# Decode attention over a long cache: P*V with V as the stationary operand, and more rows of one V chunk kept on chip

## The chip, the cores and the metric

The kernel runs on one core of a Trainium2 chip. The metric is the time of one execution in microseconds of device time; the median of three runs is used.

## The reference

Two attention blocks and two small mixer-and-MLP blocks alternate over the same x, eight batch rows of one token each. Both attention blocks read the same K and V cache, so the cache is needed twice:

```python
def _A_setup():
    B, Sq, D = 8, 1, 448
    Hq, Hkv, Sk, Dh = 16, 8, 4096, 256
...
def _A_ref(x, k_cache, v_cache, wq, wo):
    q = (lambda x, *d: x.transpose(*d))((x @ wq).reshape(B, Sq, Hq, Dh), 0, 2, 1, 3)
    k = jnp.repeat(k_cache, rep, axis=1)
    v = jnp.repeat(v_cache, rep, axis=1)
    scores = jnp.einsum("bhqd,bhkd->bhqk", q, k) * (Dh ** -0.5)
    p = _softmax(scores, axis=-1)
    o = jnp.einsum("bhqk,bhkd->bhqd", p, v)
    return (lambda x, *d: x.transpose(*d))(o, 0, 2, 1, 3).reshape(B, Sq, Hq * Dh) @ wo
...
x = x + _A_ref(_layernorm(x, axis=-1), A_k_cache, A_v_cache, A_wq, A_wo)
x = x + _B_ref(_layernorm(x, axis=-1), B_w1, B_w2, B_w3, B_w4)
x = x + _A_ref(_layernorm(x, axis=-1), A_k_cache, A_v_cache, A_wq, A_wo)
x = x + _B_ref(_layernorm(x, axis=-1), B_w1, B_w2, B_w3, B_w4)
```

The data are bf16. With S = 1 the mixer of `_B_ref` has shifts that push every row out, so only its norms, `w3`, the gelu and `w4` are computed.

## The kernel before

One batch row has 8 KV heads, each with 4096 keys of 256 values. Two KV heads form a pair `gp` (four pairs), and the K or V of a pair is cut into four chunks `c` of 1 MB: 128 partitions with 16 rows `y` of 256 bf16 values each. Every chunk lives in one of 15 places of SBUF (`places`, `slots`).

The first attention block is pass 0 (`ps == 0`), the second pass 1. A batch row's pass 1 follows soon after its pass 0, and part of the cache stays on chip between the two. Eleven chunks keep their places (`kept`: all K chunks of pairs 3 and 2, and V chunks 1 to 3 of pair 3). One more V chunk (`inner`) is put into four PSUM banks by DVE transposes (`away`, L748) and brought back for pass 1 (`back`, L755). Of one more V chunk (`part`, the first of pair 3) four of the 16 rows go into a fifth bank, `store[4]` (L960, back at L978); its load of pass 1 brings the other 12 rows, 768 KB.

`tasks` is the order of (pass, row, pair) written out by hand, and `items` cuts it into chunks: K chunks of a task alternate with the V chunks of the task before it. The main loop runs over `items`. For each item:

- A K chunk is transposed in place by DVE in three instructions (`transpose_k`, L713). Then PE makes the scores (`scores`, L728) with q as stationary operand and K moving; where two K chunks lie side by side one matmul takes both. ACT makes the exponentials and their sums (`exps`, L737), and PE and ACT turn the p of a whole task around (`transpose_p`, L764 and L771) into `ptw`.
- A V chunk goes through `pv` (L783): 16 matmuls, one for each row y, with 8 columns of `ptw` (two of them p, six zeros around) as stationary operand and the 256 values of V moving. Four rows y run at different 32-partition quadrants, and everything accumulates in one half of the PSUM bank `o` (`o_banks`), which has to be cleared before.
- Two pairs make a half. `half` (L445) sums and inverts the softmax denominators (`z_cols`, L414), copies the half bank out by ACT (L457), clears it by a DVE memset (L458), and folds the four quadrants, turns the result round and scales it in one step of four fp32 matmuls with `R` (L463). A DVE cast (L467) ends it.
- `pv_cols` (L797) is the form used for the last row's pass 1 of pairs 0 and 1: V as stationary operand, 128 columns at stride 2 for each of two column sets j, and two columns of p moving.

When an item is done its place is free (unless it is kept), and `emit_loads` issues as many of the coming loads as places allow, in the order of `items`, all on SP's queue (L700 for one chunk, L675 for two K chunks side by side). Each load waits on that queue until the last readers of its place have finished.

Everything else, output projection (L358), norms, MLP (L376), the next q (L309), is written as generators. `step` advances them between items at a pace given by the number of steps that they are said to have (`add_gen`, for instance 38 for `chain`) and by the item at which they have to be done.

Of the kernel before, what the change touches and what calls it, by code (L numbers as in the profile page):

```python
# [17 lines left out]
def kernel(  # L18
# [47 lines left out]
    part = (GP - 1, 1, 0)  # L66
    Q4 = 4 * Dh

# [23 lines left out]

    usel = consts.tile([128, 4], FP32, name="usel")
    for u in range(2):
# [6 lines left out]

    fold = consts.tile([128, 8], FP32, name="fold")
    nc.vector.tensor_reduce(
        fold[:],
        ident.rearrange("p (q n) -> p n q", q=4)[:, 0:8],
        mybir.AxisListType.X,
        ALU.add,
    )

    ptz = consts.tile([128, 520], BF16, name="ptw")  # L110
    nc.vector.memset(ptz[:], 0.0)
    ptw = ptz[:, 0:512].rearrange("p (a n w) -> p a n w", a=4, w=8)

    misc = psum.tile([128, 512], FP32, name="misc")
    ot_bank = misc[:, 256:320]
    sc = psum.tile([128, 512], FP32, name="sc")
    o_both = psum.tile([128, 512], FP32, name="o")
    o_banks = [o_both[:, 0:Dh], o_both[:, Dh : 2 * Dh]]
    store = [psum.tile([128, 512], FP32, name=f"store{n}") for n in range(5)]
    nc.vector.memset(sc[:], 0.0)  # L120
    nc.tensor.matmul(o_both[:], ptz[:, 0:128], ptz[:, 0:512], start=True, stop=True)

# [10 lines left out]

    wv = consts.tile([128, 4], FP32, name="wv")
    nc.vector.memset(wv[:, 0:3], 1.0 / D)
    nc.vector.memset(wv[0:64, 3:4], 0.0)
    nc.vector.memset(wv[64:128, 3:4], 1.0 / D)
    one = consts.tile([128, 1], FP32, name="one")
    nc.vector.memset(one[:], 1.0)
    ones = one[:].to_broadcast([128, 128])  # L140
    HTw = consts.tile([128, HC, Bn], BF16, name="HTw")
    nc.vector.memset(HTw[:], 0.0)
    low = consts.tile([128, 2, 4], FP32, name="low")
    for k, v in enumerate((1.0, (1 + EPS) ** -0.5)):
        nc.vector.memset(low[:, k], v)
        nc.vector.memset(low[0:64, k, 3:4], 0.0)
    eps2 = consts.tile([128, 2], FP32, name="eps2")
    nc.vector.memset(eps2[:, 0:1], EPS)
    nc.vector.memset(eps2[:, 1:2], EPS * EPS / (1 + EPS))
    nhalf = consts.tile([128, 1], FP32, name="nhalf")  # L150
    nc.vector.memset(nhalf[:], -0.5)
    xb = {}
    for nb in (1, Bn):
        xb[nb] = consts.tile([128, 5, nb], BF16, name=f"xb{nb}")
        nc.vector.memset(xb[nb][:, 3:5, :], 0.0)
# [47 lines left out]
    def norm(x, nb, twice):  # L203
# [15 lines left out]
        xx = room("xx", (2, 4), 0)  # L219
        nc.vector.tensor_mul(xx[:, 0], x, wv[:].unsqueeze(2).to_broadcast([128, 4, nb]))  # L220
        nc.vector.tensor_mul(xx[:, 1], xx[:, 0], x)
# [24 lines left out]
        def power(k0, k1):  # L246
            nc.gpsimd.tensor_tensor(  # L247
                rs[:, k0:k1].rearrange("p n b -> p (n b)"),
                ve[:, k0:k1].rearrange("p n b -> p (n b)"),
                nhalf[:].to_broadcast([128, (k1 - k0) * nb]),  # L250
                ALU.pow,
            )

        if twice and nb == 1:
            nc.vector.scalar_tensor_tensor(
                ve[:, :, 0], var.to_broadcast([128, 2]), 0.0, eps2[:], ALU.max, ALU.add
            )
            power(0, 2)
        else:
            if twice:  # L260
                nc.vector.tensor_scalar(
                    ve[:, 1], var, 0.0, EPS * EPS / (1 + EPS), ALU.max, ALU.add
                )
                power(1, 2)
            nc.vector.tensor_scalar(ve[:, 0], var, 0.0, EPS, ALU.max, ALU.add)
            power(0, 1)
# [147 lines left out]
    def z_cols(zall, gps):  # L414

        np_ = len(gps)
        zm = chn.tile([128, 4, np_], FP32, tag=f"zm{np_}")
        zs_t = chn.tile([128, 2], FP32, tag="zs")
        zs = zs_t[:, 0:np_]
        nc.vector.tensor_add(  # L420
            zs, zall[:, 0, gps[0] : gps[-1] + 1], zall[:, 1, gps[0] : gps[-1] + 1]
        )
        nc.vector.tensor_tensor(  # L423
            zm[:],
            zs.unsqueeze(1).to_broadcast([128, 4, np_]),
            usel[:].unsqueeze(2).to_broadcast([128, 4, np_]),
            ALU.mult,
        )
        yield
        z_ps = misc[:, 480 : 480 + 4 * np_].rearrange("p (n g) -> p n g", n=4)  # L430
        nc.tensor.matmul(z_ps, ones, zm[:], start=True, stop=True)  # L431
        yield
        rz = chn.tile([128, 4, np_], FP32, tag=f"rz{np_}")
        nc.vector.reciprocal(rz[:], z_ps)
        return rz

    def scale_o(o_ps, rz, gp, u, OT):

        h0 = 4 * gp + 2 * u
        for j in range(2):  # L440
            nc.vector.tensor_mul(
                OT[:, j, h0 : h0 + 2], o_ps[:, j, h0 : h0 + 2], rz[:, 2 * u : 2 * u + 2, 0]
            )

    def half(o_ps, zall, g8, OT):  # L445


        rz = yield from z_cols(zall, range(2 * g8, 2 * g8 + 2))

        R = chn.tile([128, 8], FP32, tag="R")  # L450
        nc.vector.tensor_mul(
            R[:].rearrange("p (g n) -> p g n", n=4),
            rz[:].rearrange("p n g -> p g n"),
            fold[:].rearrange("p (g n) -> p g n", n=4),
        )
        o_sb = chn.tile([128, Dh], FP32, tag="o_sb")
        nc.scalar.copy(o_sb[:], o_ps)  # L457
        nc.vector.memset(o_ps, 0.0)  # L458
        in_use[:] = [t for t in in_use if t is not o_ps]
        yield  # L460
        ot_ps = ot_bank[:, 32 * g8 : 32 * g8 + 16].rearrange("p (j h) -> p j h", j=2)
        for j in range(2):
            nc.tensor.matmul(  # L463
                ot_ps[:, j], o_sb[:].rearrange("p (i j) -> p j i", j=2)[:, j], R[:], start=True, stop=True
            )
        yield
        nc.vector.tensor_copy(OT[:, :, 8 * g8 : 8 * g8 + 8], ot_ps)  # L467
        yield

    in_use = []  # L470

# [188 lines left out]
    def emit_loads(most=None):  # L660
        n = 0
        while loads and places and n != most:
# [35 lines left out]
            if loads:  # L698
                z0 = Q4 if tasks[t][0] == 1 and halfway(it) else 0
                nc.sync.dma_start(dst[:, z0:], src[:, z0:])  # L700
# [51 lines left out]
    def back(slot):  # L752

        for n in range(4):
            nc.vector.transpose(  # L755
                slot[:].bitcast(U32)[:, 512 * n : 512 * n + 512], store[n][:].bitcast(U32)
            )

    def transpose_p(p_sb):

        pt_ps = misc[:, 0:128].rearrange("p (t k r) -> p t k r", t=4, k=4)
        cols = identb[:].rearrange("p (k r) -> p k r", k=4)[:, :, 0:8]
        for t in range(4):
# [7 lines left out]
        nc.scalar.copy(  # L771
            ptw[:, :, :, 6:8],
            pt_ps.rearrange("p t k (a h) -> p a (t k) h", a=4),
        )

    def pv(o_ps, v, a, gp):


        g = 2 * gp + a // 2
        for y in range(16):  # L780
            q = y % 4
            at = 128 * a + 8 * (4 * q + y // 4) + 6 - 2 * (g % 4)
            nc.tensor.matmul(  # L783
                o_ps[32 * q : 32 * q + 8, :],
                ptz[:, at : at + 8],
                v[:, y * Dh : (y + 1) * Dh],
                start=False,
                stop=(y >= 12),
                skip_group_check=True,
            )  # L790

    def pv_cols(o_ps, v, a, gp):

        g = 2 * gp + a // 2
        for y in range(16):
            for j in range(2):
                nc.tensor.matmul(  # L797
                    o_ps[:, j, 2 * g : 2 * g + 2],
                    v[:, y * Dh + j : (y + 1) * Dh : 2],
                    ptw[:, a, 4 * (y % 4) + y // 4, 6:8],  # L800
                    start=(a % 2 == 0 and y == 0 and j == 0),
# [57 lines left out]
    for idx, it in enumerate(items):  # L859
# [65 lines left out]
        else:  # L925
# [23 lines left out]
            else:  # L949
                g8 = gp // 2  # L950
                if ("o", g8) not in st:
                    while len(in_use) == 2:
                        step(10 * len(items))
                    st["o", g8] = next(t for t in o_banks if all(t is not u for u in in_use))
                    in_use.append(st["o", g8])
                pv(st["o", g8], slot, c, gp)
                if ps == 0 and inside(it):
                    away(slot)
                if ps == 0 and halfway(it):
                    nc.vector.transpose(store[4][:].bitcast(U32), slot[:, 0:Q4].bitcast(U32))  # L960
            if c == 3:
                done = pairs_done[ps, b] = pairs_done.get((ps, b), 0) + 1
                if done == 2 and ps == 0:
                    add_gen("chain", b, first_half(b, st), idx + 1, idx + (16 if b == 0 else 21), 10)
                elif done == 2:
                    add_gen("chain" if final else "last", b, first_last(b, st), idx + 1, idx + 13, 9)
                elif done == 4 and ps == 0:
                    add_gen("chain", b, chain(b, st), idx + 1, first_of[(1, b), 0] - 1, 38)
                elif done == 4 and not final:
                    add_gen("last", b, last(b, st), idx + 1, idx + (7 if b == Bn - 2 else 13), 6)  # L970
        if not (ps == 0 and stays(it)):
# [5 lines left out]
        if tasks[soon[0]][0] == 1 and halfway(soon):  # L977
            nc.vector.transpose(  # L978
                slots[where[soon]][:, 0:Q4].bitcast(U32), store[4][:].bitcast(U32)
            )  # L980
        emit_loads()
# [67 lines left out]
```

## Time and profile before

| What | Value |
|---|---|
| Time, median of 3 runs | 1098.04 us (1095.36 to 1102.22) |
| Span of the profiled execution | 1093.6 us |
| Its own time | not given by the page; the span is 4.4 us under the median |
| PE busy | 674.9 us (62%), 15063 matmuls and 15063 weight loads |
| DVE busy | 599.1 us (55%) |
| ACT busy | 125.9 us (12%) |
| Data moved | 446.80 MB, mean 409 GB/s |
| Mean granted TensorE clock | 0.593 |

Busy time is time in which at least one instruction of the engine runs, so matmuls that overlap are counted once. PE's matmuls and weight loads are separate rows (PE, PEld). A group of instructions is one line of the kernel, one operation and one shape; behind the bar stand its busy time, the mean duration of one in ns, and the idle time of the engine before it with what ended that. The 40 slices are 27.3 us each, and the digits tenths of busy time. "issue" is time in which an engine waited for nothing that the profile shows.

### The profile page before, as it was taken

How to read it: one execution, taken by the hardware profiler on the slowest of the kernel's cores; microseconds unless marked ns; L12 is line 12 of the kernel's file. 1: busy time of each engine (PE TensorE's matmuls, PEld its weight loads, DVE VectorE, ACT ScalarE, POOL GpSimd, SP SyncE). 2: the span in 40 equal slices, each digit the busy share in tenths (PEclk: the TensorE clock that was granted, in tenths of full speed). 3: DMA queues.
4: the chain of work that ended last, by engine and by line, in shares of the span. 5: the costliest groups of instructions: out<-in, count | busy, mean ns of one | idle time of the engine just before them, and what ended most of it. 6: DMA issues, size and time to landing. Idle time of an engine off the chain costs nothing. (4 is left out here: it accounts for less than half of the span.)

```text
span 1093.6 us, 32866 instructions
## 1 busy us (share of the span) xinstructions
PE 674.9 (62%) x15063; PEld 451.8 (41%) x15063; DVE 599.1 (55%) x1215; ACT 125.9 (12%) x362; POOL 16.3 (1%) x27
## 2 busy tenths in 40 slices
PE   3234568456864677446774467834776477767775
PEld 2123345334642355324552245522454244545554
DVE  4256564656366555555465564665637553585462
ACT  0001101110110111101021001201111101111110
POOL 0000000000000000000000000000000000000000
PEclk9986556655575556555566555665556555665565
DMA  9999999999999999999999999999999999999994
GB/s 356 394 427 419 416 403 420 420 416 407 418 423 419 406 417 422 423 419 402 419 422 423 420 401 418 423 421 417 411 416 421 420 398 419 421 411 409 421 417 188
DMA packets 62010, 446.80 MB, mean 409 GB/s; under 512 B 6568, under 2 KB 10544, under 8 KB 12336
## 3 DMA queue, kind: packets, MB, share of 16 engines
q1 hardware_dynamic: 61680, 444.32, 98.6%
q8 instruction: 118, 1.93, 0.7%
q10 hardware_dynamic: 192, 0.38, 0.2%
q14 instruction: 20, 0.16, 0.0%
HBM read 444.67 MB, written 0.01 MB: 407 GB/s over the span
## 5 line engine op out<-in xcount | busy, mean ns | idle before, releaser
L713 DVE STREAM_TRANSPOSE places<-places 128x512 uint32<-128x512 uint32 (+1 forms) x576 | 462.0, 858 | 263.1 <-DMA places<-in_A_k_cache_dram 262.7
L728 PE MATMUL sc<-places,qbd 128*8 128x128 bf16 (+1 forms) x6720 | 281.9, 309 | 217.8 <-DVE places L713 179.7
L783 PE MATMUL o<-places,ptw 128*8 128x256 bf16 x3968 | 241.9, 387 | 144.6 <-DMA places<-in_A_v_cache_dram 122.1
L728 PEld LDWEIGHTS <-qbd 128*8 128x8 bf16 x6720 | 161.2, 101 | 312.8 <-issue 136.8
L783 PEld LDWEIGHTS <-ptw 128*8 128x8 bf16 x3968 | 114.1, 109 | 192.2 <-issue 151.0
L737 ACT ACTIVATE p_n<-sc 128x256 bf16<-128x256 f32 x128 | 95.6, 747 | 763.1 <-PE sc L728 763.1
L309 PEld LDWEIGHTS <-wq_sb 128*128 128x128 bf16 x1152 | 36.0, 104 | 28.3 <-issue 18.4
L358 PEld LDWEIGHTS <-wo_sb 128*128 128x128 bf16 x1280 | 38.4, 102 | 19.8 <-issue 19.8
L332 DVE CAST qbd<-misc 32x64 bf16<-32x64 f32 x64 | 13.8, 216 | 55.6 <-PE misc L328 55.0
L309 PE MATMUL misc<-xb,wq_sb 128*128 128x1 bf16 x1024 | 34.5, 166 | 6.2 <-ACT ptw L771 3.2
L358 PE MATMUL misc<-OT,wo_sb 128*128 128x1 bf16 x1024 | 34.5, 165 | 1.2 <-issue 1.2
L737 ACT ACTIVATION_READ_ACCUMULATOR p_n<-sc 128x1 f32 x128 | 33.9, 265 | 0.0
L771 ACT CAST ptw<-misc 128x128 bf16<-128x128 f32 x64 | 17.4, 273 | 139.1 <-PE misc L764 79.1
L463 PEld LDWEIGHTS misc<-R,o_sb 128*128 128x128 f32 x124 | 26.1, 292 | 9.4 <-issue 8.6
L247 POOL TENSOR_TENSOR t<-t,nhalf 128x2 f32<-128x2 f32 (+2 forms) x20 | 14.0, 703 | 1064.9 <-DVE t L268 1064.9
L463 PE MATMUL misc<-R,o_sb 128*128 128x8 f32 x124 | 28.8, 342 | 0.1
L431 PE MATMUL misc<-zm,one 128*128 128x8 f32 (+1 forms) x66 | 18.5, 354 | 15.0 <-DVE zm L423 14.2
L755 DVE STREAM_TRANSPOSE places<-store 128x512 uint32<-128x512 uint32 x32 | 20.1, 684 | 10.7 <-PE sc L728 10.6
L431 PEld LDWEIGHTS misc<-zm,one 128*128 128x128 f32 x66 | 16.0, 300 | 21.5 <-issue 15.8
L376 PEld LDWEIGHTS <-w_sb 128*128 128x128 bf16 x560 | 17.2, 105 | 9.4 <-issue 9.2
L376 PE MATMUL misc<-xb,w_sb 128*128 128x1 bf16 (+1 forms) x560 | 18.5, 166 | 3.6 <-DVE xb L286 2.2
L748 DVE STREAM_TRANSPOSE store<-places 128x512 uint32<-128x512 uint32 x32 | 19.9, 690 | 0.9 <-DMA places<-in_A_v_cache_dram 0.8
(103 smaller groups left out, 241.9 us busy)
## 6 DMA issues: line engine op xcount, KB each, us to landing
places<-in_A_v_cache_dram SPq DMA_DIRECT2D x215, 1024.0 KB, 9.5
places<-in_A_k_cache_dram SPq DMA_DIRECT2D x146, 1024.0 KB, 9.9
places<-in_A_k_cache_dram SPq DMA_DIRECT2D x23, 2048.0 KB, 18.7
places<-in_A_v_cache_dram SPq DMA_DIRECT2D x8, 768.0 KB, 7.2
wo_sb<-in_A_wo_dram SPq DMA_DIRECT2D x1, 3584.0 KB, 27.5
wq_sb<-in_A_wq_dram SPq DMA_DIRECT2D x3, 1024.0 KB, 8.0
w_sb<-in_B_w_dram SPq DMA_DIRECT2D x1, 1568.0 KB
w_sb<-in_B_w_dram SPq DMA_DIRECT2D x3, 448.0 KB, 26.2
```

Source lines behind the costliest of these rows:

```text
L309: nc.tensor.matmul(q_ps[:, j * Hq + h, :], w, xbs(nb)[:, xi, :], start=(fc == 0), stop=(fc == 3),)
L358: nc.tensor.matmul(y_ps[:, fc, :], w[:, i, at : at + 128], rhs(i), start=start, stop=stop, skip_group_check=open is not None,)
L376: nc.tensor.matmul(h_ps[:, c * nb : c * nb + nb], w, xbs(nb)[:, xi, :], start=(fc == 0), stop=(fc == 3),)
L431: nc.tensor.matmul(z_ps, ones, zm[:], start=True, stop=True)
L463: nc.tensor.matmul(ot_ps[:, j], o_sb[:].rearrange("p (i j) -> p j i", j=2)[:, j], R[:], start=True, stop=True)
L713: nc.vector.transpose(w, w)
L728: nc.tensor.matmul(sc[32 * k : 32 * k + 8, 128 * x : 128 * (x + nx)], qbd[:, ep, gp].rearrange("p a h -> p (a h)"), v, start=(n == 0), sto ...
L737: nc.scalar.activation(p_sb[:, :, :, 2 * u : 2 * u + 2].rearrange("p t i x -> p x t i"), sc[:, 256 * u : 256 * u + 256].rearrange("p (x t ...
L748: nc.vector.transpose(store[n][:].bitcast(U32), slot[:].bitcast(U32)[:, 512 * n : 512 * n + 512])
L755: nc.vector.transpose(slot[:].bitcast(U32)[:, 512 * n : 512 * n + 512], store[n][:].bitcast(U32))
L771: nc.scalar.copy(ptw[:, :, :, 6:8], pt_ps.rearrange("p t k (a h) -> p a (t k) h", a=4),)
L783: nc.tensor.matmul(o_ps[32 * q : 32 * q + 8, :], ptz[:, at : at + 8], v[:, y * Dh : (y + 1) * Dh], start=False, stop=(y >= 12), skip_group ...
```

## The change

`pv` takes the form of `pv_cols`: for each of two column sets j and 16 rows y, 128 values of V at stride 2 are the stationary operand and the two columns of p move. That is 32 matmuls and 32 weight loads a chunk instead of 16 and 16, and the result lies as columns (head dimension on partitions), with start and stop of an accumulation for each chunk. A chunk of a pair has 4 output columns (two j, two heads), and the partial results of a half need 32 columns of the `o` bank instead of 256. So no clearing is needed, and `half` adds the two parts of each head (a DVE copy and an add) and multiplies by the inverse denominators; the ACT copy, the memset, `R` and the four fp32 matmuls are gone. Only one half at a time may be at work (`halves`).

The room that this leaves holds more of the `part` chunk: four rows in `store[4]` as before, three rows in the rest of the `o` bank, and four rows in a new SBUF tile `vx`, filled by an ACT copy and read by PV directly. `vx` finds its room because `ptw` shrinks to 128 columns and several small constants share one tile, `small`. The load of pass 1 brings five rows, 320 KB. The number of steps that the generators are said to have falls by two each.

```diff
-    Q4 = 4 * Dh
+    YS, YO, YX = 4, 3, 4
+    Y1 = YS + YO
+    YL = Y1 + YX
...
-    ptz = consts.tile([128, 520], BF16, name="ptw")
-    nc.vector.memset(ptz[:], 0.0)
-    ptw = ptz[:, 0:512].rearrange("p (a n w) -> p a n w", a=4, w=8)
+    ptw_t = consts.tile([128, 128], BF16, name="ptw")
+    ptw = ptw_t[:].rearrange("p (a n h) -> p a n h", a=4, h=2)
+    vx = consts.tile([128, YX * Dh], BF16, name="vx")
...
-    o_banks = [o_both[:, 0:Dh], o_both[:, Dh : 2 * Dh]]
+    o_sets = [o_both[:, 32 * k : 32 * k + 32] for k in range(2)]
+    o_rows = o_both[:, 512 - YO * 128 : 512]
...
-    def half(o_ps, zall, g8, OT):
+    def half(o_set, zall, g8, OT):
+        while halves:
+            yield
+        halves.append(g8)
         rz = yield from z_cols(zall, range(2 * g8, 2 * g8 + 2))
-        R = chn.tile([128, 8], FP32, tag="R")
-        nc.vector.tensor_mul(
-            R[:].rearrange("p (g n) -> p g n", n=4),
-            rz[:].rearrange("p n g -> p g n"),
-            fold[:].rearrange("p (g n) -> p g n", n=4),
+        parts = o_set.rearrange("p (j n a h) -> p a j n h", j=2, a=2, h=2)
+        o_t = chn.tile([128, 2, 8], FP32, tag="o_t")
+        o_v = o_t[:].rearrange("p j (n h) -> p j n h", h=2)
+        nc.vector.tensor_copy(o_v, parts[:, 0])
+        nc.vector.tensor_tensor(o_v, parts[:, 1], o_v, ALU.add)
+        in_use[:] = [t for t in in_use if t is not o_set]
+        nc.vector.tensor_tensor(
+            OT[:, :, 8 * g8 : 8 * g8 + 8],
+            o_t[:],
+            rz.rearrange("p g n -> p (g n)").unsqueeze(1).to_broadcast([128, 2, 8]),
+            ALU.mult,
         )
-        o_sb = chn.tile([128, Dh], FP32, tag="o_sb")
-        nc.scalar.copy(o_sb[:], o_ps)
-        nc.vector.memset(o_ps, 0.0)
-        in_use[:] = [t for t in in_use if t is not o_ps]
-        yield
-        ot_ps = ot_bank[:, 32 * g8 : 32 * g8 + 16].rearrange("p (j h) -> p j h", j=2)
-        for j in range(2):
-            nc.tensor.matmul(
-                ot_ps[:, j], o_sb[:].rearrange("p (i j) -> p j i", j=2)[:, j], R[:], start=True, stop=True
-            )
-        yield
-        nc.vector.tensor_copy(OT[:, :, 8 * g8 : 8 * g8 + 8], ot_ps)
+        halves.clear()
         yield
...
-                z0 = Q4 if tasks[t][0] == 1 and halfway(it) else 0
+                z0 = YL * Dh if tasks[t][0] == 1 and halfway(it) else 0
...
+    row_stores = [(0, YS, store[4][:]), (YS, Y1, o_rows)]
+    def rows_away(slot):
+        for y0, y1, t in row_stores:
+            nc.vector.transpose(t.bitcast(U32), slot[:, y0 * Dh : y1 * Dh].bitcast(U32))
+        nc.scalar.copy(vx[:], slot[:, Y1 * Dh : YL * Dh])
+    def rows_back(slot):
+        for y0, y1, t in row_stores:
+            nc.vector.transpose(slot[:, y0 * Dh : y1 * Dh].bitcast(U32), t.bitcast(U32))
...
-    def pv(o_ps, v, a, gp):
-        g = 2 * gp + a // 2
-        for y in range(16):
-            q = y % 4
-            at = 128 * a + 8 * (4 * q + y // 4) + 6 - 2 * (g % 4)
-            nc.tensor.matmul(
-                o_ps[32 * q : 32 * q + 8, :],
-                ptz[:, at : at + 8],
-                v[:, y * Dh : (y + 1) * Dh],
-                start=False,
-                stop=(y >= 12),
-                skip_group_check=True,
-            )
+    def pv(o_set, v, a, gp, kept_rows=None):
+        o_ps = o_set.rearrange("p (j g a h) -> p j g a h", j=2, g=2, a=4)
+        for j in range(2):
+            for y in range(16):
+                src, at = v, y
+                if kept_rows is not None and Y1 <= y < YL:
+                    src, at = kept_rows, y - Y1
+                nc.tensor.matmul(
+                    o_ps[:, j, gp % 2, a, :],
+                    src[:, at * Dh + j : (at + 1) * Dh : 2],
+                    ptw[:, a, 4 * (y % 4) + y // 4, :],
+                    start=(y == 0),
+                    stop=(y == 15),
+                )
...
                 if ps == 0 and halfway(it):
-                    nc.vector.transpose(store[4][:].bitcast(U32), slot[:, 0:Q4].bitcast(U32))
+                    rows_away(slot)
...
-                    add_gen("chain", b, chain(b, st), idx + 1, first_of[(1, b), 0] - 1, 38)
+                    add_gen("chain", b, chain(b, st), idx + 1, first_of[(1, b), 0] - 1, 36)
...
         if tasks[soon[0]][0] == 1 and halfway(soon):
-            nc.vector.transpose(
-                slots[where[soon]][:, 0:Q4].bitcast(U32), store[4][:].bitcast(U32)
-            )
+            rows_back(slots[where[soon]])
```

## The prediction, made before the changed kernel was run

> **What bounds the kernel now.** I read the busy shares and the DMA rows of the page first, then the windows by stage, then the chain that ended last, then the groups by shape. The DMA rows decide most of it.
>
> ```profile
> span 1093.6 us, 32866 instructions
> DMA  9999999999999999999999999999999999999994
> GB/s 356 394 427 419 416 403 420 420 416 407 418 423 419 406 417 422 423 419 402 419 422 423 420 401 418 423 421 417 411 416 421 420 398 419 421 411 409 421 417 188
> q1 hardware_dynamic: 61680, 444.32, 98.6%
> q8 instruction: 118, 1.93, 0.7%
> ```
>
> The DMA engines are busy in every slice but the last, at about 420 GB/s with a dip near 400 once in every 130 us or so, that is once a batch row. So the time is bytes over rate, and what the dips lose. Where the dips come from is seen when a batch row is cut in two, a stretch in which pass 2 and the kept chunks leave few free places, and one in which places are plentiful:
>
> ```profile
> 500.00:564.00 64.00, 50.06 (x1103) 33.63 (x1104) 34.65 (x83) 8.38 (x25) 1.26 (x2) 0.55 1.01 412
> 632.00:692.00 60.00, 45.95 (x938) 30.66 (x934) 30.47 (x76) 7.09 (x22) 1.25 (x2) 0.50 1.00 410
> 692.00:760.00 68.00, 35.17 (x758) 22.00 (x750) 40.45 (x62) 8.04 (x23) 0.00 (x0) 0.63 1.01 422
> ```
>
> The columns are PE, weight loads, DVE, ACT, POOL with their counts, then clock, DMA share, GB/s. In 632 to 692 a load lands 7.6 us (median) after its issue, in 692 to 760 21.5 us after: in the first there are some 1.5 MB on the way, in the second up to 9. Issued bytes less landed bytes, in 4 us slices of the trace, say what this costs: above 2 MB on the way the rate is 420 to 421 GB/s, at 1.4 to 1.6 MB 412, at 1.0 to 1.2 MB 397. The scarce slices add up to 476 us of the span. There the time hangs on how soon PE gives a place back.
>
> PE has a limit that is no busy share. In the chain of waits, at the densest place:
>
> ```profile
> 933.53 1.22 issue
> 934.76 0.48 PE misc L358 x13
> 935.24 0.13 PE misc L764 x4
> 935.39 0.28 ACT ptw L771
> 935.71 0.94 PE misc L358 x32
> 936.65 0.95 PE o L783 x16
> 937.61 1.77 PE misc L358 x63
> 939.38 1.59 issue
> 940.97 0.62 PE misc L358 x17
> ```
>
> Between the two "issue" gaps lie 13+4+32+16+63 = 128 matmuls with a weight load each: 256 instructions. PE's 15063 matmuls and 15063 weight loads at 64 bytes are 1.93 MB, which is the q8 row, and 1.93 MB in 118 packets is 16 KB, or 256 instructions, a packet. So these gaps are PE waiting for its next page of code. The page starts are 6.2 us apart here (934.76, 940.97), and of the 117 intervals between q8 packets 38 are under 6.6 us, in spite of a median of 8.2. I read a ceiling of 256 instructions in 6.2 us, 41 a us, while data transfers run.
>
> **The change, part by part.** *Fewer bytes.* Eight loads (768 KB, pass 2) become 320 KB: seven rows of 64 KB less, 3.67 MB in all. A packet of 6144 bytes takes 238 ns in the records; one of 2560 lies between 1792 bytes (80 ns) and 3584 bytes (146 ns), about 107 ns. 1024 packets x 131 ns / 16 engines = -8.4 us, if the engines stay fed.
>
> *PV on PE itself.* The shapes are in the trace already, since the last row of pass 2 does it at L797:
>
> ```profile
> L783 PE MATMUL o<-places,ptw 128*8 128x256 bf16 x3968 | 241.9, 387 | 144.6 <-DMA places<-in_A_v_cache_dram 122.1 <-issue 10.8 <-DVE o L458 9.3
> L463 PE MATMUL misc<-R,o_sb 128*128 128x8 f32 x124 | 28.8, 342 | 0.1
> L458 DVE MEMSET o<- 128x256 f32 x31 | 8.4, 272 | 12.3 <-ACT o_sb L457 11.1
> L797 PE MATMUL store<-ptw,places 128*128 128x2 bf16 x256 | 8.2, 166 | 2.3 <-DMA places<-in_A_v_cache_dram 2.3
> L797 PEld LDWEIGHTS <-places 128*128 128x128 bf16 x256 | 7.9, 106 | 3.1 <-DMA places<-in_A_v_cache_dram 2.7 <-issue 0.4
> ```
>
> Old: 241.9 / 248 chunks = 0.98 us. New: 8.2 / 256 = 32 ns a pair, 32 pairs, 1.03 us. That is a draw, +13 us of PE busy time in all, off the path. The Trainium skill (TensorE: Matmul & The Clock Gate, section LDWEIGHTS) speaks against this part: a weight load takes its columns over 1.2 ns, 107 ns for 128 against 7 ns for 8, which makes an estimate of 3.4 us a chunk. The L797 row has 31 ns of busy time for each such load, so the row is taken.
>
> *Instructions.* A chunk goes from 32 to 64 of them: 248 x 32 = 7936 more, less 31 x 8 for L463, so 7688 or 30 pages. As traffic a q8 packet lasts 1.06 us on one engine: 30 x 1.06 / 16 = +2.0 us (by bytes alone 1.2). As a ceiling it weighs more. 500 to 564 holds 2207 instructions, 272 of them PV matmuls: with 544 more and 24 less it needs 2727 / 256 x 6.2 = 66.0 us of its 64. 632 to 692: 1872 + 476 - 24 = 2324, 56.3 us of 60, where it was 45.3.
>
> What that costs no row shows. From below: nothing, where PE has waited for loads anyway (122.1 us before L783, 179.7 us at L728 for DVE). From above: in the scarce 476 us lie 3326 PV instructions, and as many new ones at 24.2 ns each are 80 us. To choose, I took the trace's PE start times, counted PV twice, and let a page arrive no sooner than 6.2 us after the page before it was begun: in the scarce slices PE is late by 0.56 us more than before in the mean, with peaks near 2 us. At 421 GB/s that is 0.24 MB less on the way, 1.2 instead of 1.45 MB, and by the rates above about 9 GB/s or 2.2% less over 476 us: +10 us. Just after the scarce stretch PE runs through kept chunks at full pace and the lateness grows to 5 to 9 us, where the loads on the way cover 2.5 to 4; pushing each issue back by it ends the loads about 5 us later, most of that in the last two batch rows: +4 us (0 to 9).
>
> The Trainium skill (Runtime: NRT & Kernel Launch, section Instruction fetch mechanics) also has blocks of 16 KiB fetched while the current one runs, but calls the cost of crossing mostly hidden; by that these two terms are nothing. The chain above, with 1.2 and 1.6 us of gap, says otherwise for dense stretches.
>
> *The end of a half.* The ACT copy (L457, 0.39 us), the memset and the four fp32 matmuls of L463 (28.8 / 31 = 0.93 us of PE) go; two short DVE operations on 16 columns and one product take the place of memset, R and cast. The DVE is 55% busy and gains nothing that counts. PE gets 0.93 us back, three times in a scarce stretch. None of it would be 0, all of it 8 x 3 x 0.93 = -22 us; by the same exchange rate as above, and because each lasts only a few us, -2 us.
>
> *Rows kept.* Eight times DVE moves 384 columns more out and in (0.72 us x 384/512 = 0.54 us each), and ACT copies 1024 columns: no row like it, between the 0.38 us of L457's 256 and four times that, 1.5 us. The move into the o bank also waits for PE, and the K transposes queue behind it. The place comes back later by 0 to 1.5 us, 0 to 12 us in all. SP waited for the old move only twice, 0.8 us, so +1 us.
>
> Sum: -8.4 + 2.0 + 10 + 4 - 2 + 1 = +6.6 us. The page gives the profiled execution's span alone, 1093.6 us; the median of the runs, 1098.0, is 4.4 above it, and I let that stay. 1098.0 + 6.6 = 1104.6, say 1105 us: hardly slower, within 1%. One per cent, 11 us, is about what a measurement of this kernel can tell from no change.
>
> **The rivals.** *Code pages stay hidden.* PE's slack in the scarce stretch, 14.7 us of 60, was larger than the 10.9 us added, and the fetch may start earlier when PE waits. Then -8.4 + 2.0 - 2 = -8.4 us: 1090 us. Against it: PE bunches its work, 195 instructions in 636 to 640, and waits between. A gain over 1% needs the dips to go too: 476 us at 411 instead of 421 GB/s hold 11 us, which would give 1079 at best.
>
> *PE's code becomes the bound of the scarce stretch.* This is the slower side. Each place hangs on PE's queue, and PE in turn on loads and DVE. If PE keeps up only 90% of 41 a us because of these waits, 632 to 692 needs 56.3 / 0.9 = 62.6 us and 500 to 564 needs 73.3, together 11.9 us more for two batch rows, or 45 for the seven and a half that are alike; with -8.4 + 2.0 that is 1136 us. At 95% only the second is longer, by 5.5 us, 21 in all, and 1112 us. It decides from about 93%, where the scarce stretch is longer than its transfers. Against it: places are given back at one a 1.6 us even at the ceiling, and a transfer takes 2.5.
>
> *The saved rows save nothing*, since the 320 KB load lies in the scarce stretch, where the engines already run dry. Then the -8.4 falls away: 1113 us. Loads of 8192 bytes in those slices still keep the engines at 1.00 to 1.02, so I give it little.
>
> **How the numbers follow.** Forecast, 1096 to 1109: 0.42. Pages hidden, 1081 to 1095: 0.27, a third of it below 1087. PE's code the bound, 1110 to 1140: 0.27. Rows that save nothing: 0.04. So faster by over 1%: 0.09; within 1%: 0.42 + 0.18 = 0.60, less 0.06 for the edge of the forecast towards 1110, 0.54; slower: 0.27 + 0.04 + 0.06 = 0.37. The range leaves a tenth at each end: 1087 to 1126.
>
> **What would show it.** Right: q8 near 148 packets and 2.4 MB, the DMA's total near 443.6 MB, PV rows at about 32 ns a pair; "issue" gaps before PV weight loads, ending 256 instructions apart and 6.2 us apart, over whole scarce stretches; the rate there at 400 to 405 GB/s and still 421 where places are plentiful. Wrong: scarce stretches at 412 or more with q8 packets 7 us apart (the first rival), or packets 6.2 us apart without a break and the rate below 390 (the second).

## The result, and the profile after

The changed kernel takes 1118.05 us (median of 4 runs, 1114.2 to 1120.4), the kernel before 1099.01 us (4 runs): a ratio of 1.0168, 95% interval 1.0142 to 1.0195. It is 19 us slower; 1105 were forecast. Its profiled execution is the run of 1114.2 us, with a span of 1112.3.

The page of the changed kernel, its span, rates and DMA queues:

```profile
span 1112.3 us, 40541 instructions
GB/s 359 396 426 419 401 409 385 420 408 392 395 425 420 397 417 402 424 417 394 378 424 420 420 400 397 420 421 407 413 385 422 419 397 379 422 349 406 403 420 147
DMA packets 62040, 443.62 MB, mean 399 GB/s; under 512 B 6568, under 2 KB 10544, under 8 KB 12336
q1 hardware_dynamic: 61680, 440.65, 97.4%
q8 instruction: 148, 2.42, 0.9%
```

Bytes and code pages are what was worked out: 443.6 MB, 148 packets of q8. But the dips are deeper and more of them, 385, 378, 385, 379, and one of 349 late in the run, where the kernel before had 411. Reckoned from issues and landings in slices of 4 us, with both ends of the run left out, slices with less than 2 MB on the way make up 468 us at 394 GB/s; in the kernel before they are 412 us at 411. Where more is on the way the rates are 417 and 420. So the rate fell below the 400 to 405 GB/s named as a sign of the forecast, not to the 390 of the second rival.

The groups by shape, behind the bar busy time and the mean of one in ns:

```profile
L802 PE MATMUL o<-ptw,places 128*128 128x2 bf16 x7872 | 251.4, 165 | 130.7 <-DMA places<-in_A_v_cache_dram 88.6 <-issue 35.3 <-DVE o_t L463 5.4
L802 PEld LDWEIGHTS <-places 128*128 128x128 bf16 x7872 | 236.5, 105 | 164.2 <-DMA places<-in_A_v_cache_dram 95.3 <-issue 66.3 <-DVE o_t L463 1.7
L769 ACT COPY vx<-places 128x1024 bf16<-128x1024 bf16 x8 | 8.4, 1046 | 0.4 <-issue 0.3
```

PV costs 32 ns a pair, as taken from L797. A chunk that nothing interrupts holds PE for 0.87 us in the median (from its first matmul to the first of what follows), the old form for 0.96. In total PV's busy time is 251.4 us where L783 had 241.9, and PE's is 680.8 us where it was 674.9. So PE's own time hardly grew.

What grew is seen in PE's timeline, in the kept chunks of pass 1 (start, us, line, output and inputs, idle time before):

```profile
572.41 0.96 PE L802 MATMUL o<-ptw,places 128*128 128x2 bf16 x30
575.88 0.19 PE L802 MATMUL o<-ptw,places 128*128 128x2 bf16 x2 [2.51 <-issue]
576.00 1.02 PE L732 MATMUL sc<-places,qbd 128*8 128x128 bf16 x32
576.96 0.58 PE L356 MATMUL misc<-OT,wo_sb 128*128 128x1 bf16 x16
577.40 0.99 PE L802 MATMUL o<-ptw,places 128*128 128x2 bf16 x32
578.33 1.03 PE L732 MATMUL sc<-places,qbd 128*8 128x128 bf16 x32
579.28 0.53 PE L802 MATMUL o<-ptw,places 128*128 128x2 bf16 x14
582.06 0.64 PE L802 MATMUL o<-ptw,places 128*128 128x2 bf16 x18 [2.25 <-issue]
```

From 575.88 to the next gap there are 2+32+16+32+32+14 = 128 pairs: one code page, then 2.25 us of waiting in the middle of a chunk, and the next page begins 6.2 us after this one. Of 147 intervals between q8 packets 76 are under 6.6 us (38 of 117 before). Over the whole run PE's waits that end in nothing but "issue" add up to 73.5 us, where they were 25.5. Nearly all of this is waits of over 0.7 us, 40 of them and 14 before; each ends 2.2 to 2.6 us after a q8 packet starts.

One thing in the windows misleads: the changed kernel's clock reads 1.00 throughout, because its record holds no change of the clock at all. Its shortest score matmul takes 262 ns, where the kernel before has 216 ns in its stretches of granted 1.00; the median is 308 ns in both. So the clock stayed halved.

### The profile page after: what moved, and what is told of

It reads as the page before. It is cut to its first block, busy times and chain, and to the rows that moved or that the text cites. A ratio compares the mean times of both kernels' runs of the same rounds, so it can differ in the third digit from the quotient of the medians.

```text
span 1112.3 us, 40541 instructions
## 1 busy us (share of the span) xinstructions
PE 680.8 (61%) x18906; PEld 539.7 (49%) x18906; DVE 603.0 (54%) x1229; ACT 126.2 (11%) x339; POOL 16.4 (1%) x27
## 5 line engine op out<-in xcount | busy, mean ns | idle before, releaser
L732 PE MATMUL sc<-places,qbd 128*8 128x128 bf16 (+1 forms) x6720 | 293.8, 321 | 231.0 <-DVE places L717 184.9
L802 PE MATMUL o<-ptw,places 128*128 128x2 bf16 x7872 | 251.4, 165 | 130.7 <-DMA places<-in_A_v_cache_dram 88.6
L802 PEld LDWEIGHTS <-places 128*128 128x128 bf16 x7872 | 236.5, 105 | 164.2 <-DMA places<-in_A_v_cache_dram 95.3
L732 PEld LDWEIGHTS <-qbd 128*8 128x8 bf16 x6720 | 163.8, 104 | 303.7 <-issue 144.0
L307 PE MATMUL misc<-small,wq_sb 128*128 128x1 bf16 x1024 | 35.6, 165 | 13.5 <-DVE small L274 8.5
L356 PE MATMUL misc<-OT,wo_sb 128*128 128x1 bf16 x1024 | 35.3, 165 | 11.8 <-issue 11.5
L245 POOL TENSOR_TENSOR t<-t,small 128x2 f32<-128x2 f32 (+2 forms) x20 | 14.0, 704 | 1083.9 <-DVE t L266 1083.9
L434 PE MATMUL misc<-zm_t,small 128*128 128x8 f32 x62 | 18.2, 366 | 14.3 <-DVE zm_t L425 7.3
L434 PEld LDWEIGHTS misc<-zm_t,small 128*128 128x128 f32 x62 | 15.5, 311 | 20.1 <-issue 13.0
L441 DVE RECIPROCAL rz_t<-misc 128x8 f32<-128x8 f32 x31 | 6.0, 195 | 29.0 <-PE misc L434 19.4
## 6 DMA issues: line engine op xcount, KB each, us to landing
wo_sb<-in_A_wo_dram SPq DMA_DIRECT2D x1, 3584.0 KB, 27.9
```

The source lines that it names most:

```text
L245: nc.gpsimd.tensor_tensor(rs[:, k0:k1].rearrange("p n b -> p (n b)"), ve[:, k0:k1].rearrange("p n b -> p (n b)"), nhalf.to_broadcast([128, ...
L307: nc.tensor.matmul(q_ps[:, j * Hq + h, :], w, xbs(nb)[:, xi, :], start=(fc == 0), stop=(fc == 3),)
L356: nc.tensor.matmul(y_ps[:, fc, :], w[:, i, at : at + 128], rhs(i), start=start, stop=stop, skip_group_check=open is not None,)
L434: nc.tensor.matmul(z_ps, ones, zm, start=True, stop=True)
L732: nc.tensor.matmul(sc[32 * k : 32 * k + 8, 128 * x : 128 * (x + nx)], qbd[:, ep, gp].rearrange("p a h -> p (a h)"), v, start=(n == 0), sto ...
L802: nc.tensor.matmul(o_ps[:, j, gp % 2, a, :], src[:, at * Dh + j : (at + 1) * Dh : 2], ptw[:, a, 4 * (y % 4) + y // 4, :], start=(y == 0), ...
```

## The experiments

In diffs, "..." stands for what is left out, and long calls are joined into fewer lines; where matmuls are added into a chunk's own output, the `stop` flag moves to its new last ones, which is not shown. Differences in us are between medians, each run's own against the kernel before on the same chip.

**The change of PV alone, and the rows alone.** In the first, the changed kernel keeps four rows:

```diff
-    YS, YO, YX = 4, 3, 4
+    YS, YO, YX = 4, 0, 0
...
-    row_stores = [(0, YS, store[4][:]), (YS, Y1, o_rows)]
+    row_stores = [(0, YS, store[4][:])]
...
-        nc.scalar.copy(vx[:], slot[:, Y1 * Dh : YL * Dh])
```

> The changed kernel with four rows kept as before (the loads of pass 2 are 768 KB again, no vx, nothing in the o bank): the change of PV alone. Code pages (PE gets no more than 256 instructions in about 6 us, and the new PV needs 30 pages more): about 1118 us if the seven rows saved nothing, 1126 us if they were worth their bytes (8.4 us). The rows as the cause of the loss (their moves, or a load too small to cover the next): near 1099 us.

1118.88 against 1100.14 us, ratio 1.0161 (1.0109 to 1.0213). The whole loss comes with PV, and the seven rows change nothing that can be measured: 1118.9 without them, 1118.1 with them. In the second run the kernel before loads fewer rows:

```diff
-                z0 = Q4 if tasks[t][0] == 1 and halfway(it) else 0
+                z0 = 11 * Dh if tasks[t][0] == 1 and halfway(it) else 0
```

> The kernel before, with its eight loads of pass 2 cut from 12 rows to 5 and nothing kept in their place: seven rows of one V chunk are taken from whatever the place held, so that part of PV is left out. Bytes saved alone. If they are worth their bytes: 1099 - 8.4 = 1091 us. If the stretch with few places is paced by how soon places come back: 1096 to 1099 us. Above 1099 if the small load harms.

1097.64 against 1100.14 us, 0.9978 (0.9947 to 1.0008). 3.67 MB less bring 2.5 us at the median and perhaps nothing. Its window of the stretch with few places, to be held against 60.00 us at 410 GB/s before:

```profile
632.00:692.00 60.00, 42.19 (x886) 28.08 (x890) 30.68 (x79) 6.61 (x20) 1.25 (x2) 0.50 1.00 400
```

Fewer bytes, at a lower rate. But the profiled execution is the slowest of this kernel's ten, 1104.5 us, and that of the kernel before one of its fastest, 1095.4 us; so this row does not show that the smaller load lowers the rate.

**Instructions against PE time.** Two additions to the old PV, one with many short instructions, one with few long ones:

```diff
+        for y in range(16):
+            nc.tensor.matmul(misc[0:8, 500:501], ptz[:, 128 * a : 128 * a + 8],
+                             v[:, y * Dh : y * Dh + 1], start=True, stop=True)
```

> The kernel before, with 16 idle pairs of an 8-column weight load and a one-column matmul after each PV chunk: 32 instructions more a chunk, as many as in the changed kernel, some 0.45 us of PE time more. Code pages: 148 q8 packets, 1117 to 1127 us, the loss of the changed kernel without its saved bytes. PE time or the clock as the cause: the same as the run with one long matmul instead.

1127.58 against 1100.14 us, 1.0233 (1.0185 to 1.0280).

```diff
+        nc.tensor.matmul(misc[:, 500:504], ones, usel[:], start=True, stop=True)
```

> The kernel before, with one idle fp32 matmul (128x128 weights, 4 columns) after each PV chunk: some 0.5 us of PE time more a chunk, but only 2 to 4 instructions. Code pages: 1099 to 1105 us, at most 4 q8 packets more. PE time as the cause: 1115 us or more, at or above the run with 16 idle pairs.

1117.47 against 1100.14 us, 1.0132 (1.0090 to 1.0175). PE time alone was not expected to cost 17 us. Both additions write `misc`, which DVE reads for the chain, and the trace has DVE waiting for the idle matmuls (the copy of q for 42 us, 26 us before). This alone does not explain the 17 us, for in the changed kernel, which has no idle matmuls, the same copy waits 45 us. So they were made again with zero weights, added into the chunk's own output, where no other reader is:

```diff
+            if y % 4 == 3:
+                for k in range(4):
+                    nc.tensor.matmul(o_ps[32 * k : 32 * k + 8, 0:1], ptz[:, 512:520],
+                                     v[:, y * Dh : y * Dh + 1], start=False, ...)
```

> The kernel before, with 16 pairs of a zero weight load (8 columns) and a one-column matmul between the four rounds of each PV chunk, added into the chunk's own output: 32 instructions more a chunk and only a little more PE time, since four long matmuls run while they are issued. Unlike the 16 idle pairs tried first they touch no tile that DVE reads for another purpose. Code pages alone: 148 q8 packets, 1108 to 1112 us (the 10 us that lay between the two earlier runs). If code pages are all of the loss: 1118 us. If they are none of it: 1099 to 1102 us.

1117.34 against 1100.01 us, 1.0162 (1.0106 to 1.0217): 17 us, the loss of the change. In PE's timeline a chunk with its zero pairs holds PE for 1.03 us (508.94 to 509.97) instead of 0.96.

```diff
+        for k in range(2):
+            nc.tensor.matmul(o_ps[0:8, :], ptz[:, 512:520],
+                             v[:, k * Dh : (k + 1) * Dh], start=False, ...)
```

> The kernel before, with two zero matmuls of 256 columns on one quadrant after each PV chunk, added into the chunk's own output: 0.43 us of PE time more a chunk, 4 instructions. If PE time by itself costs what the idle fp32 matmul seemed to: 1112 to 1117 us. If that run paid for DVE waiting behind the idle matmul: 1100 to 1106 us.

1108.98 against 1100.01 us, 1.0081 (1.0055 to 1.0107). PE's busy time and the q8 rows of the two, zero pairs first:

```profile
PE 702.2 (63%) x19031; PEld 506.1 (45%) x19031; DVE 598.2 (54%) x1215; ACT 126.0 (11%) x362; POOL 16.4 (1%) x27
q8 instruction: 149, 2.44, 0.9%
```

```profile
PE 742.3 (67%) x15559; PEld 512.0 (46%) x15559; DVE 599.2 (54%) x1215; ACT 125.7 (11%) x362; POOL 16.4 (1%) x27
q8 instruction: 122, 2.00, 0.7%
```

Against the 674.9 us of the kernel before, the long matmuls bring 67 us of busy PE time, and that costs 9 us (the 0.43 us a chunk of the expectation, 107 us in all, hold only at the halved clock). At that price the 27 us of the zero pairs are worth 3.6 of their 17 us. The rest, some 13 to 14 us, goes with the number of instructions. The first pair fits this price: its single fp32 matmul brings 104 us of busy time, worth 14 of the 17 us measured (10 to 19 by the interval), and its 16 pairs bring 94 us, worth 12.5 of 27, which leaves 15 for the instructions.

**Where instructions cost.** The zero pairs in one part of the PV chunks each (the diff is against the run with all zero pairs):

```diff
-            if y % 4 == 3:
+            if y % 4 == 3 and ((ps, gp) in ((0, 0), (0, 1), (1, 1))):
```

> The zero pairs only in the 92 PV chunks that fall into the stretch with few free places (pass 0 of pairs 0 and 1, pass 1 of pair 1): 2944 instructions more. If code pages cost where PE's pace gives back the places: most of the 17 us of all 248 chunks, 1109 to 1115 us. If the cost is spread by chunks: 92/248 of 17 us, 1106 us.

1102.43 against 1099.75 us, 1.0030 (1.0009 to 1.0051).

With `((1, 3), (1, 2))` in the same place:

> The zero pairs only in the 64 PV chunks of pairs 3 and 2 in pass 1, where PE runs through kept chunks at its fastest: 2048 instructions more. By the prediction's term for the lateness built up there (4 us, 0 to 9): 1102 to 1106 us. By chunks: 64/248 of 17 us, 1104 us.

1107.14 against 1099.75 us, 1.0069 (1.0043 to 1.0096).

With `((1, 0), (0, 2), (0, 3))`:

> The zero pairs only in the 92 PV chunks of the stretch in which loads wait for nothing (pass 0 of pairs 2 and 3, pass 1 of pair 0): 2944 instructions more. Code pages are hidden there: 1099 to 1101 us, the traffic of 11 or 12 pages. By chunks: 1106 us.

1102.13 against 1099.75 us, 1.0028 (1.0005 to 1.0052).

Together 12.5 us of the 17. The few chunks of the kept pairs cost most, 115 ns each against 29 and 26. PE's "issue" waits say the same: 62.6 us with the zero pairs in the kept chunks, 33.3 and 27.9 us with them in the stretches with few and with plenty of places, 25.5 us without any. The windows of the kept-chunk run around its last batch row but one show where (columns as before: PE, weight loads, DVE, ACT, POOL, clock, DMA share, GB/s):

```profile
968.00:976.00 8.00, 5.34 (x102) 3.65 (x99) 7.62 (x15) 0.98 (x3) 0.00 (x0) 0.71 0.75 266
976.00:984.00 8.00, 7.12 (x168) 4.56 (x168) 8.00 (x14) 1.06 (x3) 0.00 (x0) 0.58 0.87 304
```

The same stretch of the kernel before, and then of the changed kernel, a little later:

```profile
968.00:976.00 8.00, 6.56 (x189) 4.09 (x184) 7.50 (x10) 1.79 (x5) 0.00 (x0) 0.83 1.00 391
976.00:984.00 8.00, 2.95 (x76) 1.58 (x64) 4.17 (x5) 0.76 (x2) 0.00 (x0) 0.60 1.01 420
```

```profile
976.00:984.00 8.00, 5.17 (x156) 4.19 (x149) 7.65 (x14) 1.00 (x3) 0.00 (x0) 1.00 0.80 290
984.00:992.00 8.00, 6.00 (x177) 4.45 (x170) 7.05 (x13) 2.59 (x6) 0.00 (x0) 1.00 0.91 323
```

The DMA engines stand idle here, a share of 0.75 to 0.91. The kept chunks of the last row but one coincide with the output projection and MLP of four earlier rows (`rest`), all short pairs: PE draws a page every 6 us without a break from 940 to 970 in the changed kernel, and gives places back late. The loads that SP issued there (start, us, line, output and input):

```profile
963.95 0.33 SPq L704 DMA_DIRECT2D places<-in_A_v_cache_dram  x1
969.80 0.33 SPq L704 DMA_DIRECT2D places<-in_A_k_cache_dram  x1
974.37 0.33 SPq L704 DMA_DIRECT2D places<-in_A_v_cache_dram  x1
979.45 0.33 SPq L704 DMA_DIRECT2D places<-in_A_k_cache_dram  x1
```

They are about 5 us apart, where 1 MB takes 2.5 us at 420 GB/s; the kernel before issued seven loads between 963.25 and 975.89. Against 420 GB/s the two windows of the changed kernel lose 2.5 + 1.8 = 4.3 us, those before 0.6.

**PE time in the same chunks**, the two long zero matmuls in the kept pairs alone (against the run with long matmuls everywhere):

```diff
-        for k in range(2):
+        for k in range(2 if (ps, gp) in ((1, 3), (1, 2)) else 0):
```

> The kernel before, with two zero matmuls of 256 columns after each of the 64 PV chunks of pairs 3 and 2 in pass 1: 0.43 us of PE time more a chunk, 27 us in all, but 256 instructions instead of the 2048 that cost 7.4 us in the same chunks. If code pages are what PE lacks there: 1100 to 1102 us. If any PE time costs there: 1107 us or more.

1101.33 against 1100.67 us, 1.0012 (0.9990 to 1.0035). That is nothing that can be told from no change (-1.1 to +3.9 us), where 2048 short instructions cost 7.4 us. The two runs are a close pair: in the 64 chunks PE's own time, idle time left out, is 49.3 us in the kernel before, 59.7 us with the long matmuls (not 27 us more, as expected at the halved clock) and 60.1 us with the zero pairs. PE's idle time inside these chunks is 11.8, 8.3 and 38.2 us.

**From the other side.** The new PV with four rows kept, pages taken away and PE time put back:

```diff
-        for j in range(2):
+        cut = (ps, gp) in ((1, 3), (1, 2))
+        for j in range(1 if cut else 2):
...
+        for k in range(2 if cut else 0):
+            nc.tensor.matmul(o_both[:, 128:384], v[:, 0 : 2 * 128 : 2],
+                             v[:, k * Dh : (k + 1) * Dh], start=True, stop=True)
```

> The change of PV alone (four rows kept), with the second half of the columns (j = 1) left out in the 64 PV chunks of pairs 3 and 2 in pass 1, and two idle matmuls of 256 columns in its place: PE time the same, 1792 instructions or 7 pages less. Code pages: 7 us of the 18.7 us come back, about 1112 us. PE time or anything else of the new form: 1119 us.

1109.70 against 1100.67 us, 1.0086 (1.0055 to 1.0116): 9.0 us over the kernel before, where the change of PV is 18.7 over it. A quarter of the added instructions, gone from these chunks, takes half of the loss with it. Its q8 row has 141 packets. PE's "issue" waits fall from 74.3 us (the change of PV alone) to 26.1 us, the 25.5 of the kernel before. So the stalls that the trace shows account for about half of the loss; the other 9 us stand without them, and what makes them up is open. The zero pairs in the two other stretches cost 5 us, also with few stalls.

**Other candidates.** The clock: 32 moving columns instead of two, the further 30 overwritten later.

```diff
-    ptw_t = consts.tile([128, 128], BF16, name="ptw")
+    WN = 32
+    ptw_t = consts.tile([128, 128 + WN], BF16, name="ptw")
...
+                    o_set[:, 128 * j + 64 * (gp % 2) + 2 * a : 128 * j + 64 * (gp % 2) + 2 * a + WN],
```

> The change of PV alone (four rows kept), with 32 moving columns instead of two: the two of p and 30 more whose sums are overwritten later. Same instructions, and a pair's 27 ns hides 32 columns. The end of a half reads 16 columns out of a wider layout. If the array's activity lets the clock be granted in full for part of the time, and the halved clock costs: 1118 - 4 to 10 = 1108 to 1114 us and score matmuls of 217 ns in the trace. If only code pages cost: 1118 us, whatever the clock.

1114.33 against 1100.01 us, 1.0127 (1.0099 to 1.0155). The clock does rise (mean 0.595, shortest score matmul 216 ns), and most of the loss stays. The same layout with two columns:

```diff
-    WN = 32
+    WN = 2
```

> The kernel with 32 moving columns, its layout and all, but with two columns moving: the same instructions at the halved clock throughout. If the clock costs: 1118 to 1120 us, 4 us or more over the 1114.3 us of 32 columns. If it doesn't: 1113 to 1116 us.

1116.09 against 1100.67 us, 1.0146 (1.0110 to 1.0183). The intervals overlap: between these two the clock is worth 2 us, by the intervals anything from nothing to some 7. Against the change of PV alone, whose output lies differently, it would be 4 us. This stays open.

The end of a half, made cheap in the old kernel:

```diff
-        R = chn.tile([128, 8], FP32, tag="R")
+        R = chn.tile([128, 8], BF16, tag="R")
...
-        o_sb = chn.tile([128, Dh], FP32, tag="o_sb")
+        o_sb = chn.tile([128, Dh], BF16, tag="o_sb")
```

> The kernel before, with the fold of a half in bf16 (o_sb and R): two weight loads and two matmuls of about 0.1 us in all instead of 0.93 us of PE, 31 times. If PE time in the stretch with few places costs 17 us for 248 x 0.55 us, 26 us less of it is worth 3 us: 1096 us. If the fold lies off the path: 1099 us.

1101.81 against 1100.01 us, 1.0015 (0.9996 to 1.0035). Nothing is gained.

Bytes, where they do count: as much left out of a load in the stretch with plenty of places.

```diff
+                if tasks[t][0] == 0 and b and (gp, kv, c) == (GP - 2, 1, 0):
+                    z0 = 8 * Dh
```

> The kernel before, with eight rows of one V chunk of pair 2 in pass 0 not loaded in the seven batch rows after the first (that part of PV takes whatever the place held): 3.67 MB less, as many bytes as the seven kept rows, but in the stretch in which the DMA engines set the pace. If bytes count there and not where places are few: 1099 - 8.4 = 1091 us, against 1097.6 for the rows left out of the other stretch. If no byte counts: 1099 us.

1092.98 against 1099.75 us, 0.9935 (0.9914 to 0.9956): 6.8 us for 3.67 MB, against 2.5 for the same bytes in the other stretch; the two intervals only just touch. As it leaves work out, it is no version to use. No kernel tried does the whole work faster than the one before.

## Why the prediction was wrong, point by point

- *Fewer bytes, -8.4 us.* This step failed. Its condition, "if the engines stay fed", doesn't hold where those loads lie: -2.5 us in the old kernel (+0.9 to -5.8), nothing with the new PV (1118.1 us with the rows, 1118.9 without). The rival that said so got 0.04. Engine time was saved, 7.2 of the 8.4 us (a packet of 2560 bytes took 125 ns in the mean, not 107), but the run did not get shorter by it. What I held against it, a DMA share near 1.00, is an average; a share of 1.00 at 410 GB/s is not the 421 of a full queue. That a smaller load also leaves fewer bytes on the way to cover the next is argued, not shown.
- *PV on PE, a draw.* Right, 32 ns a pair, and 9.5 us more busy time in all where 13 were reckoned. The Trainium skill's 107 ns for a weight load of 128 columns (TensorE: Matmul & The Clock Gate, section LDWEIGHTS) is near the 105 ns that one load lasts here. But the loads overlap, with 236.5 us of busy time for 7872 of them, 30 ns each, so the estimate of 3.4 us a chunk does not come about.
- *Code pages as a ceiling.* The mechanism was right: instructions at the same PE time cost most of what the change costs. Where they cost was not. Over the scarce stretch I charged 10 us; the zero pairs there cost 2.7 us (1.0 to 5.6 by the interval). For the kept chunks I charged 4 us (0 to 9); they cost 7.4 (4.7 to 10.6). For the stretch with plenty of places I charged traffic only; it cost 2.4 (0.5 to 5.7), and why was not tried. All three at once cost 17.3, some 5 more than the sum, an excess within the intervals. That the 16 us charged for pages in all came so near is luck: the excess in the scarce stretch made up for what was missing elsewhere. The 10 us also rested on a rate that falls from 412 to 397 GB/s as the bytes on the way fall from 1.5 to 1.1 MB; reckoned again, the trace of the kernel before gives 408 to 420 at 1.4 to 1.6 MB and 407 to 418 at 1.0 to 1.2, no clear fall.
- *Pages stay hidden*, the first rival, falls: PE's "issue" waits grew from 25.5 to 73.5 us. With it falls, for this kernel, what the Trainium skill says of page crossings (Runtime: NRT & Kernel Launch, section Instruction fetch mechanics), that their cost is mostly hidden. *PE's code becomes the bound*, 1110 to 1140, holds the time, but its place was wrong: I looked for the bound in the scarce stretch and found the costliest place in the kept chunks.
- *The end of a half, -2 us.* Nothing (-0.4 to +3.9 by the interval for the bf16 fold). *Rows kept, +1 us*: not to be told from nothing.
- The sum again with what was measured: about 0 for the bytes, 13 to 14 for the instructions with their traffic, 1 for PE's 6 us more of busy time, 2 to 4 for the clock, which the prediction did not have: 16 to 19, and 19 was measured. With intervals of 5 us and more on the larger terms it closes no better than that. That only one half may be at work, and the generators' step counts, were not tried apart.

## What to carry to other kernels

Count PE's instructions, not only its busy time: stalls 256 instructions apart that no semaphore ends are the sign, and a form of matmul that is free in time but doubles the instructions is dear where PE runs dense. Ask of every byte saved in which stretch it is loaded, since where few places are free the pace can be set by how soon they come back. Dummy work has to write where nobody else reads, or it can measure waits that it made itself.

## What the runs showed of the hardware

- Where PE waited for one code page of 256 instructions (16 KB) after another, the pages began 5.7 to 6.7 us apart, 6.2 in the median of 24 cases in the changed kernel. Single q8 packets started as little as 4.7 us apart with the DMA engines fully busy, and 3.6 us apart where their share was 0.86.
- 7936 added PE instructions in 31 pages cost 17 us with 27 us of busy PE time, where 67 us of busy PE time in 992 instructions cost 9 us. In the 64 kept chunks, at the same PE time, 2048 instructions cost 7.4 us and 256 cost 0.7, within noise.
- Dense pairs of a 128-column weight load and a two-column matmul never raised the clock in the changed kernel: no score matmul under 262 ns in the whole run. With 32 moving columns and the same instructions it rose, to a mean of 0.595 and 216 ns.
- The page gives a clock of 1.00 for a run in which the clock never changed from its lower state. Durations have to be read beside it.
